# One cached-attention decode block: TensorE's loop over all four head groups, plain waits in the tail, and a two-queue store of spread rows

## The chip, the cores and the metric

The kernel runs on one NeuronCore of a Trainium2 chip. The metric is device time in microseconds (us), read from the chip. A profiled execution gives the trace; its span (first to last instruction) is shorter than the device time (669.41 against 667.4 before). Times inside a trace count from the start of the span.

The engines by their short names: PE multiplies matrices (PEld is its loading of weights, PSUM holds its results), DVE does vector work, ACT functions such as exponents, POOL a few fills, and SP issues transfers (DMA) between main memory and SBUF, the memory that the engines work on. A transfer "lands" when its data have arrived; "SP goes on" is the moment at which SP's wait for the stores ends.

## The reference, cut to what matters

```python
B, Sq, D = 4, 1, 640;  H, Sk, Dh = 32, 4096, 128;  F = 1728
h  = x + attention(layernorm(x), k_cache, v_cache, wq, wo)     # q: one token per batch row
h2 = h + (mish(layernorm(h) @ w1 + b1)) @ w2                   # output: 4 rows of 640, bf16
```

The caches are 4 x 32 x 4096 x 128 in bf16, K and V: 268 MB of the 283 MB that the kernel reads. Each byte is used once.

## The kernel before: the parts that matter

The heads are handled in 4 groups of 8, with the 4 batch rows in turn: 16 tiles of K and 16 of V, 8 MB each, go through three slots of SBUF. SP issues all big loads on one queue. DVE multiplies K by q in place, PE folds the products and does the products with V, ACT takes exponents. The programs of the engines are written apart and meet on semaphores; PE's program alone has a hardware loop.

In that loop PE's waits must be the same in each turn, so a wait in `take` subtracts what it waited for:

```python
for sem, n in want.items():
    d = n - self.seen.get(sem, 0)
    ...
    if sem in self.take:
        self.eng.wait_ge(h, d).then_inc(h, -d)    # an instruction of its own on PE's queue
    elif self.live:
        self.eng.wait_ge(h, n)                    # can ride on the next instruction
```

In before's trace the subtracting wait is an instruction of 51 ns on PE's queue (129 of them), and where two or three follow each other they start 0.15 us apart. From 640 us on PE's queue has 22 of them.

The loop has 3 turns, because the finish of a head group (`o_mm`, `l_mm`, `a_mm`) is mixed with the first tile of the next group. The fourth turn is written out a second time, without that part:

```python
for s in range(NS): fold(0, s)
with nc.tensor.Fori(0, LOOP): pe_body(0, False)   # LOOP = NHG - 1 = 3
pe_body(NHG - 1, True)                            # some 900 more PE instructions
pe_tail()
```

The tail: the four pieces of Wo, a layernorm, W1 in two pieces, the mish chain on DVE and ACT, W2 in three pieces. The last product keeps its four quarters of the output columns in the four 32-partition groups of PSUM, 4 rows in each, so that four matmuls run side by side (in before 52 of them, 333 ns each on average, took 1.96 us). One copy to SBUF, then four stores:

```python
mm(y2_ps[k * QD : k * QD + N, :], act[0:rows, j, :], w2_sb[:, j, cs], ...)      # rows 32k .. 32k+3
dv.do(lambda: v.tensor_copy(out=o_bf[:, :], in_=y2_ps), "o_bf", DV)
for q in range(CG):                                                             # SP
    load(sp, out_rows[:, q * OC : (q + 1) * OC], o_bf[q * QD : q * QD + N, :], ("out", q), "OUT")
```

The softmax here doesn't subtract the row's maximum and nothing guards it: scores larger than these inputs give would overflow.

## Time and profile before

| | before |
|---|---|
| device time, median | 669.44 us |
| span of the profiled run | 667.4 us |
| last piece of Wo: landed, first matmul on it | 650.37, 650.66 |
| `cen` (centred rows) done, first W1 matmul | 653.71, 654.00 |
| `act` started, done, first main `y2` matmul | 660.69, 660.91, 661.44 |
| `o_bf` copy starts, first store issued, SP goes on | 663.44, 663.79, 666.02 |

From the page of before: the span, two engines' busy times, the DMA row of the 40 slices (tenths busy), and two rows of the queue table (packets, MB, share of 16 engines' span). q1 is SP's queue; q8 carries PE's instructions.

```profile
span 667.4 us, 5166 instructions
PE 394.1 (59%) x2729; PEld 79.4 (12%) x1769; DVE 406.5 (61%) x250; ACT 41.0 (6%) x157; POOL 2.6 (0%) x14
...
DMA  9999999999999999999999999999999999999995
...
q1 hardware_dynamic: 6160, 283.35, 98.5%
q8 instruction: 10, 0.16, 0.1%
```

The reader is to see a stream that never stops until the last slice: the kernel is bound by its bytes, and what remains to be won is the tail. In the landing records the 8 MB tiles land one after the other from 94.6 to 637.1 us, 19.35 to 19.37 us apart but for two steps of 19.53 and 19.55.

From the timeline of before, in the tail (start, duration, engine, line, operation, out<-in; in brackets the idle time before it and what ended it):

```profile
647.75 1.76 PE L657 MATMUL y_ps<-a_t,slotB 128*128 128x4 bf16 x40
...
650.66 1.73 PE L657 MATMUL y_ps<-a_t,slotB 128*128 128x4 bf16 x40 [1.15 <-PEq L44]
...
653.53 0.18 DVE L582 TENSOR_TENSOR cen<-st,mu 128x20 bf16<-128x20 f32 x1
...
654.00 2.73 PE L657 MATMUL red<-cen,slotB 128*64 128x4 bf16 x42 [0.30 <-PEq L44]
...
660.69 0.22 DVE L646 SCALAR_TENSOR_TENSOR act<-tb,hm 128x56 bf16<-128x56 f32 x1
661.18 0.12 PEld L657 LDWEIGHTS red<-w_tail,act 64*4 64x4 bf16 x4 [1.50 <-issue]
661.21 0.30 PE L657 MATMUL red<-w_tail,act 64*4 64x160 bf16 x4 [1.35 <-PEq L44]
...
661.44 1.96 PE L657 MATMUL red<-slotA,act 128*4 128x160 bf16 x52
663.44 0.32 DVE L653 CAST o_bf<-red 128x160 bf16<-128x160 f32 x1 [2.53 <-PE red L657]
663.79 1.33 SPq L239 DMA_DIRECT2D out_dram<-o_bf  x4
```

PEq L44 as what ended a wait means: PE's own queue was busy with a wait instruction (line 44 is the subtracting one). Behind the 1.15 us before the last Wo matmuls stands a landing, which the landing records show at 650.37.

### The profile page before, as it was taken

What the parts mean: (1) busy time and instruction counts of PE and PEld (TensorE: products, weight loads), DVE (VectorE), ACT (ScalarE), POOL (GpSimd) and SP (SyncE); (2) the same over time, 40 slices, a digit from 0 to 9 for tenths busy, and PEclk for the clock granted to TensorE, in tenths of its full rate; (3) what the DMA queues carried; (4) which work ended last, traced back from release to release, by engine and by line L of the source; (5) the groups of instructions that cost most, each with busy time, mean ns of one, the idle gap of its engine ahead of it and who ended that gap; (6) DMA issues with size and microseconds to landing.
All of it is one profiled execution on the core that took longest, in us unless ns stands there. A gap on an engine that the chain in (4) does not pass through costs nothing. (4 is left out here: it accounts for less than half of the span.)

```text
span 667.4 us, 5166 instructions
## 1 busy us (share of the span) xinstructions
PE 394.1 (59%) x2729; PEld 79.4 (12%) x1769; DVE 406.5 (61%) x250; ACT 41.0 (6%) x157; POOL 2.6 (0%) x14
## 2 busy tenths in 40 slices
PE   0855748456327585847308395848426575847576
PEld 0700100101101010101100010100110010010155
DVE  1068988295058788666128798768208798849412
ACT  0200000000000010000000000000000000000011
POOL 1000000000000000000000000000000000000000
PEclk9668787879759796869557887878766878788875
DMA  9999999999999999999999999999999999999995
GB/s 378 437 440 440 433 420 409 441 440 437 429 436 436 436 436 424 424 440 436 432 432 440 436 432 432 416 440 436 433 432 436 440 436 433 428 425 440 428 396 198
DMA packets 6405, 283.55 MB, mean 425 GB/s; under 512 B 948, under 2 KB 1016, under 8 KB 1528
## 3 DMA queue, kind: packets, MB, share of 16 engines
q1 hardware_dynamic: 6160, 283.35, 98.5%
q8 instruction: 10, 0.16, 0.1%
q10 hardware_dynamic: 232, 0.01, 0.0%
q14 instruction: 3, 0.02, 0.0%
HBM read 283.35 MB, written 0.01 MB: 425 GB/s over the span
## 5 line engine op out<-in xcount | busy, mean ns | idle before, releaser
L466 DVE TENSOR_TENSOR slotA<-slotA,q_bc 128x8192 bf16<-128x8192 bf16 x32 | 140.7, 4416 | 110.9 <-DMA slotA<-in_A_k_cache_dram 110.7
L466 DVE TENSOR_TENSOR slotB<-slotB,q_bc 128x8192 bf16<-128x8192 bf16 x32 | 140.7, 4416 | 16.3 <-DMA slotB<-in_A_k_cache_dram 16.3
L667 PE MATMUL red<-slotA,ident 128*128 128x512 bf16 x480 | 141.0, 459 | 0.0
L477 DVE TENSOR_REDUCE s_f<-red 128x64 f32<-128x1024 f32 x64 | 78.1, 1220 | 96.9 <-PE red L667 96.8
L667 PE MATMUL red<-slotB,ident 128*128 128x512 bf16 x480 | 123.3, 415 | 0.0
L657 PE MATMUL red<-slotA,ident 128*128 128x512 bf16 x32 | 14.2, 445 | 119.3 <-PEq L44 119.3
L657 PE MATMUL pv<-slotC,e 128*32 128x512 bf16 x768 | 52.4, 434 | 42.7 <-PEq L44 42.7
L657 PE MATMUL red<-slotB,ident 128*128 128x512 bf16 x32 | 14.1, 441 | 87.0 <-PEq L44 87.0
L348 ACT ACTIVATE ex<-s_f 128x64 bf16<-128x64 f32 x64 | 16.4, 256 | 502.3 <-DVE s_f L477 502.3
L491 DVE TENSOR_TENSOR e<-ex,hmask 128x512 bf16<-128x512 bf16 x64 | 39.8, 682 | 0.0
L657 PEld LDWEIGHTS pv<-slotC,e 128*32 128x32 bf16 x768 | 22.5, 108 | 103.0 <-issue 89.4
L657 PEld LDWEIGHTS red<-slotA,ident 128*128 128x128 bf16 x32 | 3.2, 98 | 200.7 <-issue 200.6
L657 PEld LDWEIGHTS red<-slotB,ident 128*128 128x128 bf16 x32 | 3.2, 98 | 165.1 <-issue 165.1
L657 PEld LDWEIGHTS o_ps<-pv_sb,selo 128*32 128x32 f32 x128 | 12.7, 109 | 59.1 <-issue 59.1
L657 PE MATMUL o_ps<-pv_sb,selo 128*32 128x128 f32 x128 | 17.0, 276 | 0.0
L657 PE MATMUL pv<-slotA,e 128*32 128x512 bf16 x256 | 14.5, 380 | 0.9 <-PEq L44 0.9
L358 ACT COPY pv_sb<-pv 128x512 f32<-128x512 f32 x16 | 9.4, 585 | 75.7 <-PE pv L657 75.7
L348 ACT ACTIVATION_READ_ACCUMULATOR ex<-s_f 128x1 f32 x64 | 11.9, 186 | 0.0
L657 PE MATMUL red<-q_all,sel 32*128 32x128 bf16 x128 | 10.8, 280 | 0.8 <-PEq L44 0.8
L657 PEld LDWEIGHTS red<-q_all,sel 32*128 32x128 bf16 x128 | 10.6, 128 | 1.2 <-issue 1.2
L516 DVE RECIPROCAL rl<-misc 32x1 f32<-32x1 f32 x4 | 0.6, 150 | 16.2 <-PE misc L657 16.2
L657 PEld LDWEIGHTS pv<-slotA,e 128*32 128x32 bf16 x256 | 7.0, 97 | 22.1 <-issue 16.5
(93 smaller groups left out, 74.0 us busy)
## 6 DMA issues: line engine op xcount, KB each, us to landing
slotC<-in_A_wq_dram SPq DMA_DIRECT2D x1, 5120.0 KB, 15.1
slotB<-in_A_wo_dram SPq DMA_DIRECT2D x4, 1280.0 KB, 19.1
slotB<-in_B_w_dram SPq DMA_DIRECT2D x1, 1296.0 KB, 26.8
slotA<-in_B_w_dram SPq DMA_DIRECT2D x1, 960.0 KB, 30.3
slotB<-in_B_w_dram SPq DMA_DIRECT2D x1, 864.0 KB, 28.8
slotA<-in_B_w_dram SPq DMA_DIRECT2D x1, 800.0 KB, 32.0
slotA<-in_B_w_dram SPq DMA_DIRECT2D x1, 320.0 KB, 30.2
slotC<-in_A_v_cache_dram SPq DMA_DIRECT2D x12, 44.9
```

What stands on the lines that cost most here:

```text
L348: lambda: a.activation(out=ex[:, sl], in_=s_f[:, sl], func=ACT.Exp, scale=SCALE, accum_out=rs[:, b, s : s + 1],),
L358: lambda: a.copy(out=pv_sb[:, :, :].rearrange("p r d -> p (r d)"), in_=pv[:, :]),
L466: lambda: v.tensor_tensor(out=t, in0=t, in1=q_bc[:, hg, b, :].unsqueeze(1).to_broadcast([P, RS, Dh]), op=ALU.mult,),
L477: lambda: v.tensor_reduce(out=s_f[:, s * RS : (s + 1) * RS], in_=red[:, k : k + 2, :].rearrange("p k (r c) -> p (k r) c", c=CW), axis=AX.X ...
L491: lambda: v.tensor_tensor(out=e[:, sl, :], in0=ex[:, sl].unsqueeze(2).to_broadcast([P, RS, G]), in1=hmask[:, :].unsqueeze(1).to_broadcast( ...
L516: dv.do(lambda: v.reciprocal(out=rl[:, :], in_=l_ps), ("rl", hg), DV)
L657: lambda: nc.tensor.matmul(out_, lhsT=lhsT, rhs=rhs, start=start, stop=stop, skip_group_check=skip),
L667: return t.add_instruction(mybir.InstMatmult(name=nc.get_next_instruction_name(), engine=mybir.EngineType.PE, ins=[t.lower_ap(rhs), t.lowe ...
```

## The change

Its intent: less code on PE, by running all four groups through the loop, with a group's finish at the head of the next turn (in the first turn the finish works on filler data that nothing uses); cheaper waits in the tail, where nothing repeats and no wait has to subtract; and a store that goes out at once on two queues instead of four times on one. For the last, each store takes 8 rows from partitions at one even distance. So the activations are spread to 32 columns, 7 zeros after each, and the output rows come to lie 8 partitions apart. In the W1 part, one product that waits for no weights (b1) moved ahead of the wait for the second piece of W1.

```diff
+    def freeze(self):
+        self.base = dict(self.seen)
 ...
-            if sem in self.take:
+            if sem in self.take and self.base is None:
 ...
-                self.eng.wait_ge(h, n)
+                low = self.base.get(sem, 0) if sem in self.take else 0
+                self.eng.wait_ge(h, n - low)
 ... (act, h_hi, h_lo become parts of one zeroed tile; ROW = 8)
+    spread = sb("spread", (P, 2 * DC + FC, N, ROW), BF16, tail, topA)
-                out=act[:, :, :], in0=tb3[:, :, :], scalar=-0.5, in1=hm2[:, :, :],
+                out=act[:, :, :, 0], in0=tb3[:, :, :], scalar=-0.5, in1=hm2[:, :, :],
-                    y2_ps[k * QD : k * QD + N, :], act[0:rows, j, :],
+                    y2_ps[k * QD : (k + 1) * QD, :],
+                    act[0:rows, j, :, :].rearrange("p n r -> p (n r)"),
 ... (SP calls store(sp, 0), ACT store(ac, 1); the four stores on SP go)
+    def store(p, h):
+        c, n = CG // 2, D // 2
+        p.need("o_bf")
+        load(p, out_rows[:, h * n : (h + 1) * n].rearrange("b (k o) -> k b o", k=c),
+             o_bf[h * P // 2 : (h + 1) * P // 2 : ROW, :], ("out", h), f"OUT{h}")
 ... (pe_body: finish moved to its head; pe_tail calls pe.freeze() first)
+        fold(i, 0)
+        o_mm(i - 1)
+        l_mm(hg - 1)
+        fold(i, 1)
+        fold(i, 2)
+        a_mm(hg - 1)
+        fold(i, 3)
 ...
-                with nc.tensor.Fori(0, LOOP) as _:
+                with nc.tensor.Fori(0, NHG) as _:
 ...
-        pe_body(NHG - 1, True)
         pe_tail()
```

More of the change, by code (lines that the diff above doesn't have):

```diff
@@ L27, in restart @@
         self.log = []
+        self.base = None
+    def freeze(self):
+        self.base = dict(self.seen)
     def need(self, *keys):
@@ L107 @@
     EPS = 1e-5
-    LOOP = NHG - 1
     ctx.enter_context(tc.tile_critical(name="k", no_gpsimd_drain=True))
@@ L113 @@
     WSEM = ["WQ", "WT"] + [f"W{k}" for k in range(9)]
-    for s in ["PE", "DV", "DVP", "DVA", "AC", "ACP", "PO", "KA", "KB", "VA", "VC", "X", "S", "OUT"] + WSEM:
+    for s in ["PE", "DV", "DVP", "DVA", "AC", "ACP", "PO", "KA", "KB", "VA", "VC", "X", "S", "OUT0", "OUT1"] + WSEM:
         book.handles[s] = tc.alloc_semaphore(s)
@@ L192 @@
     b1s = sb("b1s", (P, FC, N), FP32, tail, topA)
-    h_hi = sb("h_hi", (P, DC, N), BF16, tail, topA)
-    h_lo = sb("h_lo", (P, DC, N), BF16, tail, topA)
+    ROW = QD // N
+    spread = sb("spread", (P, 2 * DC + FC, N, ROW), BF16, tail, topA)
+    h_hi, h_lo, act = (
+        spread[:, j0:j1, :, :] for j0, j1 in ((0, DC), (DC, 2 * DC), (2 * DC, 2 * DC + FC))
+    )
     h1 = sb("h1", (P, FC, N), FP32, tail, topA)
@@ L200 @@
     hm2 = sb("hm2", (P, FC, N), FP32, tail, topA)
-    act = sb("act", (P, FC, N), BF16, tail, topA)
     o_bf = sb("o_bf", (P, OC), BF16, tail, topA)
@@ L239, in load @@
         p.do(lambda: p.eng.dma_start(out=dst, in_=src), key, sem, 16)
+    def store(p, h):
+        c, n = CG // 2, D // 2
+        p.need("o_bf")
+        load(
+            p, out_rows[:, h * n : (h + 1) * n].rearrange("b (k o) -> k b o", k=c),
+            o_bf[h * P // 2 : (h + 1) * P // 2 : ROW, :], ("out", h), f"OUT{h}",
+        )
     def sync_prog():
@@ L285, in sync_prog @@
             load(sp, w2_sb[:, j0:j1, :], w2_v[:, j0:j1, :], ("w2", j0), f"W{NHG + 2 + k}")
-        sp.need("o_bf")
-        for q in range(CG):
-            load(
-                sp, out_rows[:, q * OC : (q + 1) * OC], o_bf[q * QD : q * QD + N, :],
-                ("out", q), "OUT",
-            )
-        sp.need(("out", CG - 1))
+        store(sp, 0)
+        sp.need(("out", 0), ("out", 1))
     def pool_prog():
@@ L311, in pool_prog @@
         po.do(lambda: g.memset(ones_d[:, :], 1.0 / D), "ones_d", "PO")
+        po.do(lambda: g.memset(spread[:, :, :, :], 0.0), "spread", "PO")
         po.do(lambda: g.memset(zeros[:, :], 0.0), "zeros", "PO")
@@ L341, in act_prog @@
             )
+        ac.need("ident")
+        ac.do(
+            lambda: a.copy(
+                out=pv_sb[:, :, :], in_=ident[:, :].unsqueeze(1).to_broadcast([P, RQ, Dh])
+            ),
+            ("pvc", -1), "ACP",
+        )
         def exp(i, s):
@@ L384, in act_prog @@
         )
+        store(ac, 1)
     def dve_prog():
@@ L458, in dve_prog @@
         dv.do(lambda: v.tensor_copy(out=xT[:, :, :], in_=tpx[:, :, :]), "xT", DVP)
+        dv.do(lambda: v.memset(rsm[:, :, :], 1.0), ("rsm", -1), DVP)
         dv.need(("qc", NHG - 1), "hmask")
@@ L540, in dve_prog @@
             hg, b = divmod(i, N)
-            last = hg > 0 and b == 0
             mult(i, 0)
@@ L545, in dve_prog @@
             mult(i, 2)
-            if last:
+            if b == 0 and hg:
                 norm(hg - 1)
+            elif b == 0:
+                dv.do(lambda: v.memset(om[:, :, :], 0.0), ("om", -1), DVP)
             reduce(i, 1)
@@ L550, in dve_prog @@
             reduce(i, 2)
-            if last:
+            if b == 0 and hg:
                 heads(hg - 1)
@@ L600, in dve_prog @@
         )
-        dv.do(lambda: v.tensor_copy(out=h_hi[:, :, :], in_=st[:, 0, :, :]), "h_hi", DV)
+        dv.do(lambda: v.tensor_copy(out=h_hi[:, :, :, 0], in_=st[:, 0, :, :]), "h_hi", DV)
         dv.need("std2", "b1b")
@@ L613, in dve_prog @@
             lambda: v.tensor_tensor(
-                out=h_lo[:, :, :], in0=st[:, 0, :, :], in1=h_hi[:, :, :], op=ALU.subtract
+                out=h_lo[:, :, :, 0], in0=st[:, 0, :, :], in1=h_hi[:, :, :, 0], op=ALU.subtract
             ),
@@ L767, in a_mm, with pe_body @@
             )
-    def pe_body(hg, last):
+    def pe_body(hg):
         i = hg * N
+        fold(i, 0)
[5 more added lines that the diff above has]
+        fold(i, 3)
         fold(i + 1, 0)
@@ L784, in pe_body @@
         pv_mm(i + 3)
-        if not last:
-            fold(i + 4, 0)
-            o_mm(i + 3)
-            l_mm(hg)
-            fold(i + 4, 1)
-            fold(i + 4, 2)
-            a_mm(hg)
-            fold(i + 4, 3)
     def pe_tail():
@@ L803, in pe_tail @@
         hg = NHG - 1
+        pe.freeze()
         wo_mm(0)
@@ L823, in pe_tail @@
         for c0, c1 in zip(W1S, W1S[1:]):
-            pe.need(("w1", c0))
             if c1 == DC:
@@ L830, in pe_tail @@
                 )
+            pe.need(("w1", c0))
             for j in [FM] + list(range(FM)):
@@ L846, in pe_tail @@
                     mm(
-                        y2_ps[k * QD : k * QD + N, :].rearrange("b (m c) -> b c m", c=DC)[:, c, :],
-                        part[:, c, :], ident[:, k * QD : (k + 1) * QD], False, False,
+                        y2_ps[k * QD : (k + 1) * QD, :].rearrange("b (m c) -> b c m", c=DC)[:, c, :],
+                        part[:, c, :, :].rearrange("p n r -> p (n r)"), ident[:, k * QD : (k + 1) * QD], False, False,
                     )
@@ L872, in pe_prog @@
         pe_setup()
-        for s in range(NS):
-            fold(0, s)
+        pe.need("selo", "xT")
         logs = []
-        for hg in range(LOOP):
+        for hg in range(NHG):
             pe.log = []
             if live and hg == 0:
-                with nc.tensor.Fori(0, LOOP) as _:
-                    pe_body(0, False)
+                with nc.tensor.Fori(0, NHG) as _:
+                    pe_body(0)
                 pe.live = False
             else:
-                pe_body(hg, False)
+                pe_body(hg)
             logs.append(pe.log)
```

## The prediction

The sum is 0.85 for the stores, 0.5 for the waits and 0 to 0.2 for the code, less 0 to 0.15 for the spreading, about 1.4. What point 3 says of columns can be read in before's trace: at the granted clock of 0.50 four matmuls of 512 columns (`pv`, up to 640.55 us) start every 427 ns and four of 160 (`y2`) every 133 ns, 0.83 ns per column in both. That 32-column weight loads hide there, and the sizes given in point 3 and with the risks, were estimates.

> **What bounds the kernel.** The DMA. The queue table gives the SP queue 98.5% of the 16 engines' span; PE is busy 59%, DVE 61%. In the list of SP's issues every slot refill is queued while one or two 8 MB tiles are still to come: K2 is issued at 62.2 us, V0 before it lands near 75. From issue and landing records I estimate 9 us or more of slack at each refill, so a few us more or less on an engine inside the four head groups cost nothing. Only the tail is open.
>
> **The tail now** (timeline and landing records): PE done with the third Wo piece 649.5, idle; last Wo piece lands 650.38, PE starts 650.66; st 652.43; cen ends 653.71, first half of W1 has landed 653.68, PE starts 654.00; PE-bound to 659.1 (60 ns each pair, b1s 0.6); mish chain to 660.91; PE's first y2 matmul 661.21, the main ones 661.44 to 663.4 (W2's pieces land 658.7, 661.1, 661.9, in time); o_bf to 663.76; four stores issued by SP, one each 0.35, the first at 663.79, the last at 664.83; SP goes on at 666.02; end 667.4.
>
> **What the change does.**
> 1. Stores, four on one queue to one on each of two: the last issue moves up 1.04 us. ACT's issues looked slower at the start (0.57 against 0.41), and the pattern is longer; I take 0.2 back. Gain 0.85. [...]
> 2. Tail waits: a wait-and-subtract is an instruction of its own on PE's queue, 0.15 apart. A plain wait rides on the next weight load (st to PE took 0.05; cen to PE 0.29; act to PE 0.30, then 0.22 to the main y2 matmuls). At the last Wo piece 0.15 is saved but swallowed by W1's landing at 653.68; there 0.2 is saved; at act and W2 together 0.3. Gain 0.5.
> 3. Activations spread over 32 columns: y2 runs four matmuls in 133 ns, set by 160 columns at the granted half clock; a 32-column weight load hides there. Estimate 0 to +0.15.
> 4. Loop over all four groups: a first turn with dummy finish (o_ps matmuls 1.1 us, misc 0.2 and 0.6, a DVE memset), all in slack. The last exit now stands before the tail; compare-and-branch took 0.08 to 0.23, hidden by PE's 1.15 idle. [...] Smaller code: 10 instruction packets (0.16 MB) become perhaps 5; at most 0.2 us. Gain 0 to 0.2.
> 5. b1s before the wait for W1's second half: that landed 656.10, before PE needed it: 0.
>
> Sum: about 1.4 us, all in the tail; 669.44 to 668.0.
>
> **What would show it.** From y2's end to SP's going on, 2.6 falls to about 1.7 us; act to the main y2 matmuls, 0.53 to 0.25; the last Wo and W1 land where they did, within 0.3 us; y2's matmuls keep 2 us.
>
> **What would make it wrong.** [...]weight loads of 32 columns not hidden (up to +0.5); ACT's store much later than SP's; DMA rate varying by run (0.1% is 0.6 us).

## The result, and the profile after

The changed kernel took 668.08 us (median of 4, 667.80 to 668.16) against 669.43 for before in the same rounds: ratio 0.9978, interval 0.996 to 0.9995. That is 1.35 us by the medians. (A ratio here is the mean time of one kernel's runs over the mean of the other's of the same rounds, so it is not quite the ratio of the medians.) The total came out as forecast, 668.0. The parts did not.

The page of after:

```profile
span 666.3 us, 5193 instructions
PE 398.1 (60%) x2747; PEld 81.0 (12%) x1787; DVE 407.2 (61%) x252; ACT 41.6 (6%) x158; POOL 3.3 (0%) x15
...
q1 hardware_dynamic: 6138, 283.35, 98.7%
q8 instruction: 7, 0.11, 0.1%
```

The timeline of after, the same places:

```profile
648.39 3.32 PE L679 MATMUL y_ps<-a_t,slotB 128*128 128x4 bf16 x80
...
652.86 0.18 DVE L604 TENSOR_TENSOR cen<-st,mu 128x20 bf16<-128x20 f32 x1
...
653.09 2.74 PE L679 MATMUL red<-cen,slotB 128*64 128x4 bf16 x42
...
659.78 0.41 DVE L668 SCALAR_TENSOR_TENSOR spread<-tb,hm 128x56 bf16<-128x56 f32 x1
660.24 0.11 PEld L679 LDWEIGHTS red<-w_tail,spread 64*32 64x32 bf16 x4 [1.40 <-DVE spread L668]
660.24 0.32 PE L679 MATMUL red<-w_tail,spread 64*32 64x160 bf16 x4 [1.24 <-DVE spread L668]
...
660.49 1.92 PE L679 MATMUL red<-slotA,spread 128*32 128x160 bf16 x52
662.47 0.33 DVE L675 CAST o_bf<-red 128x160 bf16<-128x160 f32 x1 [2.29 <-PE red L679]
662.82 0.66 SPq L246 DMA_DIRECT2D out_dram<-o_bf  x1
662.83 0.64 ACTq L246 DMA_DIRECT2D out_dram<-o_bf  x1
```

Three things are to be seen. PE goes through the third and the last Wo piece without a gap (80 matmuls in one row; 40 and a gap before). The `act` operation takes 0.41 us where it took 0.22. And each store takes 0.65 to issue, where SP took 1.33 for four. The tail as a sum, each term read between the two traces:

| stretch of the chain | before | after | gain | forecast |
|---|---|---|---|---|
| first matmul on the last Wo piece | 650.66 | 649.98 | 0.68 | 0 to 0.2, put down to smaller code |
| `cen` done to first W1 matmul | 0.29 | 0.06 | 0.23 | 0.2 |
| from there to the start of `act` | 6.69 | 6.69 | 0 | 0 |
| `act` operation | 0.22 | 0.41 | -0.19 | 0 to -0.15, expected on PE |
| `act` done to main `y2` matmuls | 0.53 | 0.30 | 0.23 | 0.3 |
| `y2` matmuls | 2.00 | 1.98 | 0.02 | |
| first store issued to SP going on | 2.23 | 2.04 | 0.19 | 0.85 |
| rest | | | 0.02 | |
| span | 667.44 | 666.26 | 1.18 | 1.4 |

So the right total is the sum of two misses of about the same size: the store won 0.66 less than forecast, and the last Wo piece came 0.5 to 0.7 sooner than forecast. That they cancelled is luck: nothing in the forecast made one depend on the other. The experiments are about these two.

A first reading of the second one comes from the landing records. The records show 16 landings for each of these loads, one, as I take it, from each of the 16 DMA engines. These are the 16 landings of the third and of the last Wo piece, in order (us):

```
before, third  644.45 .46 .48 .65 .76 645.03 .10 .72 .97 .99 646.05 .16 .22 .23 .34 .35
before, last   647.54 .55 .57 .74 .85 648.12 .20           649.06 .09 .15 .26 .31 .33 .43 .44   650.37
after,  last   647.67 .68 .69 .69 .72 .73 .75 .76 648.26 .96 649.08 .16 .31 .32 .38 .67
```

Add 3.09 to the first row and you get the second, but for one: the part due at 648.81 (645.72 + 3.09) is missing, and there is one at 650.37, 1.56 later. PE started on the piece only after the 16th part (650.66 after 650.37), so the piece is 0.93 late. Just before, at 647.98, the records show a packet of 16 KB on q8, PE's instruction queue, which took 1.09 us. In after there is no packet on q8 between 179 and 651 us. The same kind of step, 1.5 to 1.7 us for one of 16, is in before after its other late packets on q8 (552.7, 588.7 and 641.1). There it struck a part that was ahead of the slowest by about as much, and no piece as a whole landed more than 0.03 late. The two longer steps of the big tiles (19.53 and 19.55) each have a packet on q8 inside them, at 119.4 and 180.1.

### The profile page after: what moved, and what is told of

It reads as the page before. It is cut to its first block, busy times and chain, and to the rows that moved or that the text cites. A ratio compares the mean times of both kernels' runs of the same rounds, so it can differ in the third digit from the quotient of the medians.

```text
span 666.3 us, 5193 instructions
## 1 busy us (share of the span) xinstructions
PE 398.1 (60%) x2747; PEld 81.0 (12%) x1787; DVE 407.2 (61%) x252; ACT 41.6 (6%) x158; POOL 3.3 (0%) x15
## 5 line engine op out<-in xcount | busy, mean ns | idle before, releaser
L689 PE MATMUL red<-slotB,ident 128*128 128x512 bf16 x480 | 125.7, 421 | 0.0
L679 PE MATMUL red<-slotB,ident 128*128 128x512 bf16 x32 | 14.2, 444 | 85.6 <-PEq L49 85.6
L679 PE MATMUL red<-slotC,lnT 128*32 128x512 bf16 x40 | 4.3, 615 | 10.0 <-PEq L49 10.0
```

The lines of the kernel that those rows point to most:

```text
L679: lambda: nc.tensor.matmul(out_, lhsT=lhsT, rhs=rhs, start=start, stop=stop, skip_group_check=skip),
L689: return t.add_instruction(mybir.InstMatmult(name=nc.get_next_instruction_name(), engine=mybir.EngineType.PE, ins=[t.lower_ap(rhs), t.lowe ...
```

## The experiments

Theory F: a fetch of PE's code sets one of 16 DMA engines back by 1.56 us in a stream without gaps, and costs time when it strikes one without that much lead. The rival, R: the landing moved by chance, or through the waits or PE's own timing. For the store: theory P, the 8-row form is slow to issue; rival Q, two queues at once hold each other up.

| run | median us | before, same rounds | ratio |
|---|---|---|---|
| loop_only | 668.35 | 669.38 | 0.9984 |
| waits_only | 668.58 | 669.38 | 0.9988 |
| compact_2x2 | 667.58 | 669.38 | 0.9974 |
| spread_one_queue | 668.63 | 669.38 | 0.9990 |
| loop_only_padded | 669.48 | 669.42 | 1.0000 |
| spread_2x2 | 668.53 | 669.42 | 0.9988 |
| compact_4sp | 667.84 | 669.42 | 0.9976 |
| after_again | 668.09 | 669.42 | 0.9980 |
| adjacent8_wrong | 668.12 | 669.34 | 0.9982 |
| gathered | 667.54 | 669.34 | 0.9968 |
| compact_2x2_again | 667.60 | 669.34 | 0.9976 |

The three groups ran on three chips; half the width of each ratio's interval is about 0.0014 (0.9 us), so single ratios are weak and the traces beside them matter. Every kernel but adjacent8_wrong gave the right result.

### loop_only: the loop without the other parts

```diff
 (from the changed kernel)
-        pe.freeze()
-    spread = sb("spread", ...)          # act, h_hi, h_lo compact again, rows 32k .. 32k+3
-        store(sp, 0) ... store(ac, 1)   # four stores on SP again
```

> Before with the loop change alone (4 turns, finish at the head of the next turn, dummy first finish); subtracting tail waits, compact activations, four stores on SP as before. Theory F (code fetch): in before, one 16 KB fetch of PE code at 648.0 us holds up one of the 16 DMA engines, so 15 sixteenths of the last Wo piece have landed by 649.44 and the last at 650.37. Fewer PE instructions mean fewer fetches: 7 on the PE queue instead of 10, no straggler over 0.4 us, last Wo piece lands about 649.7, first W1 half about 652.9; time falls by about 0.7 us (668.7). Rival R (the landing difference is variation of the run, or comes from the waits): landing stays near 650.4 and the time near 669.4.

Measured: 668.35. The last Wo piece landed at 649.58, its last part 0.24 behind the one before, the first W1 half at 652.72. The span was 0.85 below before's, and 0.79 of it is there by the first W1 matmul (653.21 against 654.00). From its page, and from its timeline:

```profile
q8 instruction: 7, 0.11, 0.1%
```

```profile
648.33 3.27 PE L672 MATMUL y_ps<-a_t,slotB 128*128 128x4 bf16 x75
```

(The window cuts off the first 5 of the 80.) F holds as forecast, and R in the form "chance" would need this run, after and the next one to fall the right way each. The b1 move came with this kernel and did nothing: from the first W1 matmul to `h` 5.13 us here, 5.14 before.

### waits_only: before with the plain waits alone

```diff
 (from before)
-            if sem in self.take:
+            if sem in self.take and self.base is None:
+        pe.freeze()                     # first line of pe_tail's work
```

> Before with the merged tail waits alone (code of the loop, activations and stores as before). F: still 10 PE fetches, last Wo piece lands near 650.4 with a straggler of about 0.9 us, first W1 half near 653.7. Waits: from cen to PE 0.05 instead of 0.29 (but W1's landing then binds: 0.2 won), from act to the main y2 matmuls 0.30 instead of 0.53. Time about 669.0 (-0.45). If the waits moved the landing (rival), last Wo lands near 649.7 and the time is 668.4 or less.

Measured: 668.58, span 0.64 below before. The straggler is there again: landings of the last Wo piece up to 649.46, then one at 650.44, after a packet on q8 at 648.30; by the third piece's landings that part was due at 648.74, so here the step is 1.70. I had expected 10 packets; the page has 11, because the one at 661.60 comes only after the span in before, at 668.37. From its page, and from its timeline, where the plain wait now lets the profile name the landing:

```profile
q8 instruction: 11, 0.18, 0.1%
```

```profile
650.49 1.76 PE L663 MATMUL y_ps<-a_t,slotB 128*128 128x4 bf16 x40 [0.50 <-DMA slotB<-in_A_wo_dram]
```

So the waits are not what moved the landing. They won a little more than forecast: 0.05 instead of 0.29 from the landing to the matmul, 0.10 instead of 0.29 from `cen` to W1, 0.28 instead of 0.53 from `act` to the main `y2` matmuls. Of the first I had said that W1's landing would swallow it; it did not, since W1's half landed at 653.53, before `cen` was done (653.56).

### loop_only_padded: the code put back, without the work

```diff
 (from loop_only, in PE's setup, where PE waits for data)
+        for _ in range(220):
+            mm(o_full[:, 0:N], ident[:, :], ident[:, 0:N], True, True)
 ...
+        for _ in range(244):            # and once more before the loop
+            mm(o_full[:, 0:N], ident[:, :], ident[:, 0:N], True, True)
```

> loop_only plus 464 pairs of weight load and 4-column matmul of no use in PE's setup, where PE waits for Wq and for the first product (6.4 to 16 us, 32 to 41 us)[...]. Theory F (each 16 KB code fetch sets one DMA engine back by 1.56 us; it costs only if that engine had less lead than that): 10 or more PE fetches again, one of them between 645 and 650 us; if it hits an engine within 1.5 us of the last, the last Wo piece lands up to 0.9 later than in loop_only (650.4 against 649.6) and the time is 668.8 to 669.3; if it hits a leading one, landing and time stay as in loop_only (668.35). Either way one landing per fetch moves by about 1.56. Rival R (the loop's form itself or the removed PE work makes the landing earlier): no landing moves with a fetch, time 668.35.

Measured: 669.48, as slow as before (669.42) and 1.1 us slower than loop_only. There are 11 packets on q8, one at 646.03. From its page, and from its timeline:

```profile
q8 instruction: 11, 0.18, 0.1%
```

```profile
651.04 1.73 PE L672 MATMUL y_ps<-a_t,slotB 128*128 128x4 bf16 x40 [1.49 <-PEq L49]
```

And the landings of the third and of the last Wo piece, listed as above:

```
padded, third  644.61 .65 .76 .82 .97 645.39 .65 .70 646.09 .18 .33 .39 .42 .44 .58 .71
padded, last   647.70 .75 .85 .91 648.06 .48 .74 .80         649.27 .42 .50 .52 .54 .68 .82   650.75
```

646.09 + 3.09 = 649.18 is missing, 650.75 stands in its place: 1.57 later, and the piece is 0.93 late. The code added does nothing that the tail waits for, and it ran before 50 us. This settles it for F: with the same loop, only filler work in the setup and with it the number and place of the fetches changed, and the whole gain of the loop was lost. It agrees with all thirteen traces: the three with a packet on q8 at 646.0 to 648.3 (before, waits_only, loop_only_padded) have the last part of the last Wo piece 0.93 to 0.99 behind the one before, the ten without have it at most 0.29 behind. (The last V tile landed 0.25 later than in loop_only, so about a quarter of a microsecond of the 1.1 came on the way.) That it is one and the same engine that falls back is inferred from the 15 other landings keeping step; the records do not name the engine.

### compact_2x2 and spread_one_queue: the form of the store, and the queues

```diff
 compact_2x2 (from the changed kernel): nothing spread, four 4-row stores, two on SP, two on ACT
+        for q in (2 * h, 2 * h + 1):
+            load(p, out_rows[:, q * OC : (q + 1) * OC], o_bf[q * QD : q * QD + N, :], ("out", q), f"OUT{h}")
 spread_one_queue (from the changed kernel): both 8-row stores on SP
-        store(ac, 1)
+        store(sp, 1)                    # in SP's program, after store(sp, 0)
```

> After with the spreading undone: activations in 4 columns, four stores of 4 rows, two on SP and two on ACT. Theory P (pattern): the 8-row store with two runs of partitions takes 0.65 to issue and 1.2 to 1.5 to its first packet; a 4-row store takes 0.35 and 0.8. Then from the first issue to SP's going on 1.6 us instead of 2.04, and the act operation takes 0.22 instead of 0.41; time about 667.4 (0.65 below after). Rival Q (two queues at once hold each other up): issues take 0.65 here too, 2.0 us or more from first issue to SP's going on; time 667.9, only the act part is won.

> After with both 8-row stores on SP, one after the other. Theory P (pattern): each issue still takes about 0.65, the second starts 0.7 after the first, SP goes on 2.4 to 2.5 us after the first issue instead of 2.04: time about 668.5 (+0.4). Rival Q (two queues at once): alone on its queue an issue takes 0.35 and 0.8 to its first packet, SP goes on 1.6 us after the first issue, time about 667.7.

Measured: compact_2x2 667.58, spread_one_queue 668.63. From their timelines, compact_2x2 first:

```profile
659.35 0.22 DVE L665 SCALAR_TENSOR_TENSOR act<-tb,hm 128x56 bf16<-128x56 f32 x1
...
662.16 0.66 SPq L244 DMA_DIRECT2D out_dram<-o_bf  x2
662.16 0.66 ACTq L244 DMA_DIRECT2D out_dram<-o_bf  x2
```

```profile
663.02 1.23 SPq L246 DMA_DIRECT2D out_dram<-o_bf  x2
```

Two 4-row stores on each of two queues took 0.66 together on each, with both queues at work: Q falls. Alone on SP, the first 8-row store still took 0.66 to issue (the second 0.53) and landed 1.69 after its start, to the hundredth what it took beside ACT's in after. So the long issue is the form's, not the company's. `act` is back at 0.22 once it writes side by side. From first issue to SP's going on, compact_2x2 took 1.82; I had expected 1.6. The difference is on ACT's queue: its second store landed 1.40 after its issue, SP's second 1.17. Whether that is ACT or the company is not shown, since no run has a store on ACT alone (see spread_2x2).

### spread_2x2 and adjacent8_wrong: what in the form is slow

P had put it down to the two-level pattern of 8 rows. In spread_2x2 the stores have 4 rows, but rows 8 partitions apart. In adjacent8_wrong the 8-row stores read 8 adjacent partitions. Its output is wrong, which doesn't matter for the time.

```diff
 spread_2x2 (from the changed kernel): four 4-row stores
+            load(p, out_rows[:, q * OC : (q + 1) * OC], o_bf[q * QD : (q + 1) * QD : ROW, :], ...)
 adjacent8_wrong (from the changed kernel)
-            o_bf[h * P // 2 : (h + 1) * P // 2 : ROW, :], ("out", h), f"OUT{h}",
+            o_bf[h * P // 2 : h * P // 2 + CG // 2 * N, :], ("out", h), f"OUT{h}",
```

> After with four 4-row stores (two on SP, two on ACT) in place of two 8-row ones, spreading kept. Pattern theory: from first issue to SP's going on 1.82 us as in compact_2x2 (2.04 in after); the act operation keeps 0.41. Time 667.85, between compact_2x2 and after. If rows 8 partitions apart were what made the issue slow, 2.0 us or more and 668.1.

> Wrong result on purpose: the changed kernel, its two 8-row stores reading 8 adjacent partitions (the wrong rows) instead of 8 partitions that lie 8 apart; nothing else changes. Since a 4-row store of rows 8 apart also took 0.61 to 0.74 to issue, theory D (the distance of the partitions makes the issue slow) expects issues of 0.3 to 0.4, SP's store landed 1.2 after its issue instead of 1.69, ACT's 1.45 instead of 1.95, and 1.55 us from first issue to SP's going on; time 667.6. Rival T (the two-level pattern of the 8-row store is slow too): issues stay at 0.65, 2.04 us, time 668.1.

Measured: spread_2x2 668.53, slower than after and a miss: I had expected 667.85. Its four issues took 0.61 to 0.74 each, and from first issue to SP's going on it took 2.78 us where I had expected 1.82; the alternative that I had named, rows 8 apart are slow to issue, is what came. Here it was SP's stores that landed late, 2.13 and 1.97 after their issue, and ACT's sooner, 1.75 and 1.67: the late one of two stores issued at the same time is not always ACT's, so a part of Q stays open for the landing. adjacent8_wrong took 668.12 and 2.13 us from first issue to SP's going on, a miss for theory D, formed after spread_2x2. The timelines, spread_2x2 first:

```profile
662.39 1.48 SPq L246 DMA_DIRECT2D out_dram<-o_bf  x2
662.40 1.33 ACTq L246 DMA_DIRECT2D out_dram<-o_bf  x2
```

```profile
662.70 0.76 SPq L246 DMA_DIRECT2D out_dram<-o_bf  x1
662.70 0.75 ACTq L246 DMA_DIRECT2D out_dram<-o_bf  x1
```

So neither P nor D is the whole. The distance between partitions alone (4 rows) makes the issue about twice as long, and so does something in the store of 8 adjacent rows. There three things changed at once against the plain store: the two-level pattern, 8 rows in place of 4, and, by the landing records, fewer parts (3 entries per store in place of 5); no run tells them apart. Only the plain form, 4 adjacent partitions and one row pitch, took 0.27 to 0.35. Why either is slow on the issuing side, no run shows, and none tried 8 compact rows in two runs of 4 partitions.

### compact_4sp and after_again: what the spreading and the two queues are worth together

```diff
 compact_4sp (from the changed kernel): loop and plain waits stay; compact, four stores on SP
 after_again: no edit
```

> Loop change and merged waits only: compact activations, four stores on SP as before. From first issue to SP's going on 2.23 us as in before, the act operation 0.22. Additive theory: loop 0.85 and waits 0.6 to 0.7 of the span, so 667.9 to 668.0, which is no slower than after: spreading and two-queue store together win nothing (0.19 lost at act, 0.19 won at the store). If the store part of the change won what was forecast (0.85), this run would be at 668.7 or later.

> The changed kernel unaltered, on the same chip as the three above, so that they can be compared: 668.0 to 668.2; 7 PE fetches, last Wo piece at 649.7, 2.04 us from first issue to SP's going on.

Measured, on one chip: compact_4sp 667.84, the changed kernel 668.09. The store took 2.23 us from first issue to SP's going on in the one and 2.05 in the other, and `act` 0.22 and 0.41. As expected, the spreading pays 0.19 at `act` for the 0.18 that the two queues win at the end. The kernel without that part is no slower.

### gathered and compact_2x2_again: one store from one tile

```diff
 gathered (from compact_2x2): the last copy in four, by two engines, into 4 rows of 640
+        gather(v.tensor_copy, dv, (0, 1), "o_v", DV)
+        gather(a.copy, ac, (2, 3), "o_a", "AC")
+        load(sp, out_rows[:, :], o_rows[:, :], "out", "OUT0")
```

> compact_2x2 with the last copy cut into four (DVE copies two quadrants of y2, ACT two, each 4 rows of 160) into one tile of 4 rows of 640, stored by one DMA from SP. The copies take 0.5 instead of 0.33; one store of 4 adjacent partitions lands 1.17 after its issue (as each of SP's did), so from issue to SP's going on 1.25 instead of 1.82. Expected 0.3 to 0.4 below compact_2x2: 667.2. If the waits for two engines and ACT's copies cost more than 0.8 together, no faster than compact_2x2.

> compact_2x2 unaltered, on the same chip, to compare: 667.5 to 667.7, 1.82 us from first issue to SP's going on.

Measured: gathered 667.54, compact_2x2 667.60. The timeline of gathered:

```profile
662.68 0.59 ACT L250 CAST o_rows<-red 4x160 bf16<-4x160 f32 x2 [3.50 <-PE red L678]
662.68 0.66 DVE L250 CAST o_rows<-red 4x160 bf16<-4x160 f32 x2 [2.24 <-PE red L678]
663.37 0.35 SPq L244 DMA_DIRECT2D out_dram<-o_rows  x1
```

From the start of the copy to SP's going on it took 2.01 us, against 2.17 in both runs of compact_2x2 (2.39 in after, 2.58 before). A single plain store landed 1.30 after its issue. So it wins 0.16 there, half of what I had expected, because the two copies in a row took 0.66 and not 0.5, and from the issue to SP's going on it took 1.32 and not 1.25. The times of the two overlap (666.89 to 667.87 and 667.37 to 668.36), so which is faster is not settled. Their medians lie 0.5 us below the changed kernel's (668.08 and 668.09, not timed in the same rounds), and their ratios to before, 0.9968 to 0.9976, below its 0.9978 and 0.9980, though the intervals overlap; what speaks for a real gain is in the traces (0.19 at `act`, 0.22 and more at the store).

## Why the prediction was right or wrong

The time held, by luck: 668.0 was forecast and 668.08 measured, because two terms were wrong by about the same amount in opposite directions. Point by point:

- **Bound by DMA, only the tail open: right.** Most 8 MB tiles land 19.36 us apart in both kernels, and the last V tile at 637.07 before and 637.29 after. After has one step of 19.64 in the second half of its stream, with a packet of 8 KB on q14 (another instruction queue) inside it, at 473.7; the work added inside the loop (dummy finish, memsets) shows nowhere.
- **Tail waits, 0.5: right.** The two places gave 0.23 each in after; alone, in waits_only, the part was worth 0.64 of span.
- **Stores, 0.85: wrong, the term was mis-sized.** It measured 0.19. The step that failed is "the pattern is longer; I take 0.2 back". I moved the last issue up by 1.04 us and kept the duration of a 4-row store. The 8-row spread store took 0.66 to issue instead of 0.35 and landed 1.69 (SP) and 1.95 (ACT) after its issue, instead of 1.17. So of the 1.04, 0.52 went to the form, 0.26 to the later landing on ACT's queue and about 0.07 to small steps such as SP's second wait; 0.19 was left. From the end of `y2` to SP's going on it took 2.39, where I had said 1.7. With the plain form two issuing engines saved 0.41 (2.23 to 1.82 in compact_2x2). The change gave half of that back, for a form whose issue took about twice as long.
- **Spread activations, 0 to 0.15 on PE: right in size, wrong in place.** PE hid the 32-column weight loads (`y2` 2.00 and 1.98 us). What cost 0.19 was DVE: 56 results per partition written 16 bytes apart took 0.41 instead of 0.22, and compact_2x2 took it back. The two writes of 20 results into the same spread tile grew too, from 0.17 to 0.21 and from 0.15 to 0.23, off the chain. No run tried a distance other than 2 and 16 bytes, so why the distance costs DVE time is not shown.
- **Loop and smaller code, 0 to 0.2: wrong, the term was mis-sized, and so was "the last Wo and W1 land where they did, within 0.3 us".** They landed 0.70 and 0.80 sooner. I had counted the fetches as bytes at the mean rate (0.08 MB, 0.2 us). But here a packet of 16 KB set back one of 16 parts, and PE started on the piece only when its slowest part had landed. It cost that part 1.56 us (1.57 in loop_only_padded, 1.70 in waits_only), and the piece was late by what that part did not have in hand: 0.93 in before and again in loop_only_padded; in loop_only and after no packet came there. PE itself was not shown waiting for code; the data stream was what paid.
- **The loop's exit, hidden: right.** Compare-and-branch took 0.08 at 641.4 us, beside matmuls in flight. In before PE jumped back at 214.8 and 370.7 us over some 890 recorded instructions, and the records show no packet on q8 between 180.1 and 552.7 us.

What binds next: in the seven traced kernels where PE ran without a gap into the last Wo piece (after, after_again, spread_one_queue, compact_4sp, adjacent8_wrong, compact_2x2_again, gathered), its first matmul there came 6.75 to 6.76 us after the end of the last product with V, whatever the landing. Over all runs that product took from 4.95 us (loop_only_padded) to 6.29 (gathered). One row each for before and after, from the windows view (stretch, length, busy time and count by engine, then granted clock of PE, DMA share, GB/s):

```profile
636.00:644.00 8.00, 6.79 (x104) 3.81 (x104) 0.00 (x0) 1.46 (x2) 0.00 (x0) 0.72 1.00 417
```

```profile
636.00:644.00 8.00, 6.57 (x85) 3.31 (x86) 0.00 (x0) 0.70 (x2) 0.00 (x0) 0.63 1.00 419
```

PE got 0.72 of its clock there before and 0.63 after, and did the product with V in 5.27 and in 5.80 us. The shares are means: the clock records of the traces hold only 0.5 and 1.0 there, and full from 640.55 before and from 641.86 after; four matmuls of that product started every 427 ns at half clock and every 216 at full, in both traces. What sets the moment of the change is not shown. That part of the tail therefore differs from run to run; no experiment was made on it.

## What to carry to other kernels

When a DMA stream has no gaps, count the code fetches as transfers in it: here a fetch set back one of a load's 16 parts by 1.56 us, and PE started on the load only after that part (650.66 after 650.37), so look at the single landings of a piece, not only at the last. Before splitting a small store over queues, keep it in the form that issues fastest; here four plain 4-row stores on two queues were 0.22 us quicker than two clever ones, and the layout that made the clever ones possible cost DVE as much as they won. A forecast that hits the total still has to be checked term by term: two of these terms were off by 0.5 to 0.7 us and cancelled.
